# One total order of a sequence-mixing and dense kernel replaced by another

## The chip, the cores and the metric

The kernel runs on one core of one Trainium2 chip. The metric is the device time of one execution in microseconds, and of several runs the median. TensorE (PE in the profile, its weight loads PEld), VectorE (DVE), ScalarE (ACT), GpSimd (POOL) and SyncE (SP, which here only issues DMAs) each work through a list of instructions of their own; semaphores tie the lists together.

## The reference

One sequence of S = 2048 positions with D = 640 channels goes through a residual block with a long convolution, and then through a residual dense block with F = 1728 hidden columns. All inputs are bf16.

```python
def _A_ref(q, k, v, shift_k, ssm_k, ssm_D):       # q is layernorm(x)
    k_shift = sum of k moved down by t, times shift_k[:, 3 - t], t = 0..3
    kv = k_shift * v
    y = irfft(rfft(kv, 4096) * rfft(ssm_k, 4096))[:2048]    # along S, per channel
    y = y + kv * ssm_D
    return q * y

def _B_ref(x, w1, b1, w2):
    h = x @ w1 + b1
    return (h * tanh(softplus(h))) @ w2           # mish

x = A_q
h = x + _A_ref(_layernorm(x), A_k, A_v, A_shift_k, A_ssm_k, A_ssm_D)
h2 = h + _B_ref(_layernorm(h), B_w1, B_b1, B_w2)
return h2
```

## The kernel before

**How work is cut.** The code builds a list of 660 operations. Each has a name, the engines that may do it, the operations that it depends on and, if it writes PSUM, a buffer. A buffer is one of four banks of 128 x 1024 f32, and an operation that takes a bank must wait until the last reader of the bank's earlier contents is done. Nothing is planned at build time: the string `ORDER` at the top of the file holds every name once, in one total order. `s2kpe_84@3` means that the product s2kpe_84 writes bank 3; `y0:d` means that y0 is done by VectorE; a letter left out means the first engine that the operation allows. `_ordered` turns the string into the list that is emitted:

```python
for tok in ORDER:
    tok, _, slot = tok.partition("@")
    name, _, eng = tok.partition(":")
    o = by_name[name]
    o.eng = _LETTER[eng] if eng else o.engs[0]
    if o.psum is not None:
        o.psum.slot = int(slot)
```

Each engine gets its operations in this order and does them in this order; between engines only the semaphores count. So a place in the string decides three things: what stands ahead of an operation on its own engine, whose bank it waits for, and, for a DMA, what stands ahead of it on its queue.

**Head.** `d_dr`, `d_cst` and `d_sk` (L271, L269, L270) are three small loads that ACT issues: the filter's direct term, a table of constants, the shift filter. `warm` (L284) makes ACT load its activation table. `wm` (L292) is nine products on zeros on TensorE. `cfpe` (L304) spreads the shift filter over the partitions, a product that needs d_cst and d_sk; `coef` (L309) copies it and `wsh0` to `wsh3` (L317) make weights from it.

**Loads.** SP issues them (L325): `d_n` (five, the long filter ssm_k), `d_k`, `d_v`, `d_g` (eight pieces of a DFT table), `d_x` (four pieces of x), `d_t2m`, `d_a12`, `d_w10` to `d_w14` (rows of w1), and at L491 and below `d_w2a`, `d_w2b`, `d_w2c` (w2).

**The convolution** is a DFT made of products with small tables.
- The filter: `dadd` (L370, DVE or POOL) adds the direct term to sample 0, `k1pe` (L376) transposes one of five blocks, `k1ev` copies it out of PSUM.
- `s1kpe` (L396, L397), 5 x 4 of them, is the first DFT stage of the filter: 16 products of a weight tile of 64 columns each, half into partitions 0 to 63, half into 64 to 127. `s1kev` copies out. `s2kpe_f` and `s2kev_f` (L422) are the second stage, six frequencies a time, with weight tiles of 128 columns.
- The input: `ktpe` (L341), `ktev`, `ktsh` (L345) transpose k and move it; `kspe` (L357, L358) multiplies by the wsh and so shifts; `kv` (L362, DVE) multiplies by v. `s1vpe`, `s1vev`, then `s2v0pe`, `s2v1pe`, `s2v2pe` and their copies are the same two stages for kv.
- `sw` (L450) are ten DMAs from SBUF to SBUF that exchange the real and imaginary rows of the filter's spectrum; `pr` (L461, DVE) multiplies the two spectra.
- `i1pe` (L479) and `i1ev` are the first stage of the inverse. `i2a`, `i2b` (for token tiles 0 to 3, in two parts) and `i2pe` (L531) are the second, one for each of 16 tiles of 128 tokens.

All copies out of PSUM named `...ev` and `y` go through one helper, `ev`: L261 if ACT does them, L263 if DVE does.

**The first norm** of tile t is `ln1_t` (L510, L511, DVE: two partial statistics and their union), `ln1pt` (L515 to L517, POOL: add eps, power -1/2, product) and `lnxt` (L522 on ACT, or L524 on POOL).

**Between the two blocks**, for each tile t: `y` copies the convolution out of PSUM (128 x 640), `wb` (L538, DVE) multiplies by the normed x, `h` (L540) adds the residual, `bn` (L544, L545) takes the second norm's statistics, `pow` (L549, L550, POOL) its power, `hc` (L559, DVE) applies it. Then the tile is transposed: tiles 0 and 1 on TensorE (`trpe`, L569, and the copy `trev`), all others by a DMA transpose that SP issues (`tr`, L573). Seven buffers hold hc, so hc of tile t waits for the transpose of tile t - 7.

**The dense block** works in five units of 256, 256, 512, 512 and 512 tokens. `m1peu_f` (L598, and L605 for the last 64 columns of F) multiplies unit u by two 128-column chunks of w1; `hbu_f` (L620, ACT) is the mish on the way out of PSUM; `m2pet` (L663, and L671 for the last 64 rows of two tiles at a time) multiplies tile t by w2; `rest` (L688) adds the residual and `d_outt` (L692) stores. The last tile is done in two parts, m2pe15a and m2pe15b (L685 for the addition of its parts, of 384 and 256 columns). Unit u needs the transposes of all its tiles: unit 2 needs tr4 to tr7, unit 3 tr8 to tr11, unit 4 tr12 to tr15. `w2z` (L495, POOL) clears half of two rows of w2.

**DMAs of SP** go out in the order of the string, with eight semaphores in rotation: each waits for the landing of the one eight earlier.

The place of an operation in the whole string, seen on each engine, is what the change touches. On TensorE, 160 of 214 operations stand ahead of the first m1pe, and m1pe2_3 (the first product of unit 2, in both orders) has 180 ahead of it.

Of the kernel before, what the change touches and what calls it, by code (L numbers as in the profile page):

```python
# [30 lines left out]
ktpe0_3 ktpe0_2 s1kev1_2 ktpe2_0@3 ktpe2_3 ktpe2_2 d_v2 ktpe2_1 ktpe0_1 ktev2 ktpe1_0@1 ktev0:a ktpe1_1 ktpe1_3 ktpe1_2 s1kpe3_3@0 d_g5 ktev1 ktsh2
s1kpe4_0@3 s1kev3_3 s1kpe1_1@2 ktsh0 s1kev4_0:d d_v3 s1kpe4_2@1 wsh0 s1kev1_1 s1kpe3_0@0 s1kev4_2:d s1kpe2_3@3 s1kev3_0 d_g3 ktpe4_0@2 ktpe4_2 ktpe4_3
s1kev2_3 ktsh1 ktpe3_0@1 ktpe4_1 ktpe3_3 ktev4 ktpe3_1 ktpe3_2 s2kpe_6@0 s2kpe_12@3 ktev3 s2kev_6 kspe0_0@2 s2kev_12 s2kpe_18@0 kv0_0 ktsh3 kspe2_0@1
s2kev_18 ktsh4 s2kpe_42@3 kv2_0 kspe3_0@2 s2kev_42 s2kpe_96@0 kv3_0 s2kpe_24@1 s2kev_96 kspe4_0@3 s2kev_24 kspe1_0@2 kv4_0 s2kpe_108@0 kspe1_1@1 kv1_0
s2kev_108 s2kpe_72@3 kspe0_1@0 d_x1 s2kev_72 kv1_1 d_x0 s2kpe_66@2 s2kpe_102@3 s2kev_66 kv0_1 kspe4_1@1 s2kev_102 s2kpe_120@2 kv4_1 kspe3_1@0
s2kev_120 s2kpe_126@3 kv3_1 s2kpe_78@1 s2kev_126 s2kpe_0@2 s2kev_78 s2kpe_114@3 s2kev_0:d s2kpe_36@0 s2kev_114 s2kpe_54@1 s2kev_36:d s2kpe_84@2
s2kev_54 s2kpe_60@3 s2kev_84 ln1_0 kspe2_1@1 s2kev_60 s2kpe_48@0 kv2_1 ln1p0 s1vpe0_2@2 s2kev_48 s1vpe1_1@3 s1vev0_2:d s1vpe2_1@1 d_x2 s1vev1_1
s1vpe1_0@0 d_x3 s1vev2_1 s1vev1_0:d s1vpe4_3@2 s1vpe3_2@3 s1vev4_3 s1vpe0_0@1 s1vev3_2:d s1vpe2_2@0 s1vev0_0 s2kpe_90@2 s1vpe1_2@3 s1vev2_2 s2kev_90:d
s1vpe0_3@1 s1vev1_2 s1vpe1_3@0 s1vev0_3:d s1vpe0_1@2 s1vev1_3 s1vpe3_0@3 s1vev0_1:d s1vpe4_1@1 s1vev3_0 s2kpe_30@0 s1vev4_1:d s2v0pe_0@2 s2kev_30
s2v0pe_48@3 s2v0ev_0 ln1_1 sw1_0 s1vpe2_0@1 s2v0pe_64@0 sw1_1 s2v0ev_48 lnx0:p s1vev2_0:d s2v0pe_112@2 sw0_0 ln1p1 s2v0ev_64 sw4_0 s2v0pe_32@3  # L40
s2v0ev_112:d s2v0pe_80@1 sw3_1 s2v0ev_32 s1vpe3_1@0 lnx1:p sw0_1 ln1_2 s1vpe4_0@2 s2v0ev_80 sw3_0 s1vpe3_3@3 sw4_1 ln1_3 s1vev3_1 ln1p2 s1vpe2_3@1
sw2_0 s1vev4_0 s1vev3_3:d sw2_1 s1vpe4_2@0 lnx2:p s1vev4_2 s2v0pe_96@2 pr1_64 ln1p3 s2v0pe_16@3 s2v0ev_96 s2v2pe_32@0 s1vev2_3:d lnx3:p s2v0ev_16
s2v2pe_80@2 pr1_96 s2v2ev_32 s2v2pe_112@1 s2v2pe_64@3 s2v2ev_112 pr1_0 s2v2pe_48@0 s2v2ev_64 s2v2pe_0@1 pr0_96 s2v2ev_0 s2v2pe_16@3 pr1_32 s2v2ev_16
s2v1pe_96@1 pr0_64 s2v2ev_48 i1pe1_1@3 s2v2ev_80 s2v2pe_96@0 pr3_0 s2v1ev_96 i1pe1_2@2 pr3_32 i1ev1_1 s2v1pe_64@1 pr0_32 s2v2ev_96 s2v1pe_0@3 i1ev1_2
pr0_0 s2v1pe_32@0 s2v1ev_0 pr3_64 i1pe1_3@2 d_w14 s2v1ev_64 d_w10 i1pe0_2@3 pr3_96 d_w11 s2v1ev_32 d_w12 i1pe0_1@1 pr4_0 d_w13 i1ev1_3 d_t2m i1pe3_3@0
i1ev0_1 pr2_96 i1pe3_1@2 i1ev3_3 pr2_64 i1pe3_0@1 i1ev0_2 i1pe0_3@0 pr2_0 i1ev3_0 i1pe0_0@3 pr2_32 i1ev3_1 i1pe3_2@1 i1ev0_3 pr4_96 i1pe2_0@2 i1ev0_0
# [687 lines left out]
```

## Time and profile before

| | before |
|---|---|
| median of 3 runs | 225.16 us (225.13 to 225.98) |
| the profiled execution's span | 223.5 us |
| busy: PE / PEld | 214.0 us (96%) / 157.6 us (70%) |
| busy: DVE / ACT / POOL | 133.2 us (60%) / 133.0 us (59%) / 58.9 us (26%) |
| DMA moved | 30.98 MB, mean 139 GB/s |
| share of the chain that ended last | PE 70%, DVE 13%, DMA 9%, ACT 4% |

The busy time of an engine is the time in which it had an instruction at work. The chain that ended last follows from the last instruction back to whatever released each step. The shares are averages over very different stages: convolution first, dense block after about 99 us. So the views of a stage say more than this table.

### The profile page before, as it was taken

What the parts mean: (1) busy time and instruction counts of PE and PEld (TensorE: products, weight loads), DVE (VectorE), ACT (ScalarE), POOL (GpSimd) and SP (SyncE); (2) the same over time, 40 slices, a digit from 0 to 9 for tenths busy, and PEclk for the clock granted to TensorE, in tenths of its full rate; (3) what the DMA queues carried; (4) which work ended last, traced back from release to release, by engine and by line L of the source; (5) the groups of instructions that cost most, each with busy time, mean ns of one, the idle gap of its engine ahead of it and who ended that gap; (6) DMA issues with size and microseconds to landing.
All of it is one profiled execution on the core that took longest, in us unless ns stands there. A gap on an engine that the chain in (4) does not pass through costs nothing.

```text
span 223.5 us, 6119 instructions
## 1 busy us (share of the span) xinstructions
PE 214.0 (96%) x2645; PEld 157.6 (70%) x2650; DVE 133.2 (60%) x232; ACT 133.0 (59%) x182; POOL 58.9 (26%) x120
## 2 busy tenths in 40 slices
...
GB/s 181 390 413 409 412 374 121 143 239 93 375 415 69 258 331 290 124 0 62 1 0 62 84 123 91 118 0 0 3 0 59 59 3 0 0 56 6 76 54 49
DMA packets 19563, 30.98 MB, mean 139 GB/s; under 512 B 10704, under 2 KB 14928, under 8 KB 18768
## 3 DMA queue, kind: packets, MB, share of 16 engines
...
q8 instruction: 21, 0.34, 0.7%
q10 hardware_dynamic: 336, 0.12, 0.2%
...
q0 software_dynamic: 96, 0.00, 0.0%
...
## 4 chain that ended last, share of the span: by engine, by line
PE 70%; DVE 13%; DMA 9%; ACT 4%; issue 2%; SPq 1%; POOL 1%; DVEq 0%
PE ps L663 26%; PE ps L598 25%; DVE ks L461 6%; DMA ks<-in_B_w_dram 4%; DMA ks<-ks 3%; PE ps L396 3%; PE ps L422 3%; ACT uv L261 3%; DMA ks<-in_A_ssm_k_dram 3%; PE ps L341 2%; PE ps L376 2%; DVE ks L263 2%; PE ps L357 2%; DVE ra L362 1%; PE ps L397 1%
## 5 line engine op out<-in xcount | busy, mean ns | idle before, releaser
L620 ACT ACTIVATE ks<-ps,b1s 128x512 bf16<-128x512 f32 (+1 forms) x69 | 36.1, 610 | 42.8 <-PE ps L598 30.3
L663 PE MATMUL ps<-ks 128*128 128x320 bf16 (+2 forms) x420 | 58.4, 299 | 0.0
L598 PE MATMUL ps<-G 128*128 128x512 bf16 (+1 forms) x320 | 57.0, 336 | 0.3
L688 DVE TENSOR_TENSOR rb<-ps,rb 128x640 bf16<-128x640 f32 x15 | 11.7, 816 | 68.9 <-PE ps L671 66.5
L663 PEld LDWEIGHTS <-ks 128*128 128x128 bf16 x420 | 40.6, 98 | 17.2 <-issue 1.3
L598 PEld LDWEIGHTS <-G 128*128 128x128 bf16 x325 | 31.3, 98 | 24.4 <-issue 1.1
L261 ACT CAST uv<-ps 128x1024 bf16<-128x1024 f32 x49 | 45.2, 1197 | 0.0
L261 ACT CAST ks<-ps 128x960 bf16<-128x960 f32 (+3 forms) x49 | 39.8, 905 | 8.1 <-PE ps L397 5.0
L461 DVE TENSOR_TENSOR ks<-ks,uv 128x2048 bf16<-128x2048 bf16 x20 | 23.1, 1225 | 0.7 <-DMA ks<-ks 0.7
L422 PEld LDWEIGHTS <-G 128*128 128x128 bf16 x512 | 20.9, 96 | 3.1 <-issue 2.5
L479 PE MATMUL ps<-a_t,ks 128*128 128x128 bf16 x320 | 18.8, 219 | 0.4 <-DVE ks L461 0.3
L479 PEld LDWEIGHTS <-ks 128*128 128x128 bf16 x320 | 18.3, 113 | 0.7 <-DVE ks L461 0.6
L422 PE MATMUL ps<-uv,G 128*128 128x64 bf16 (+1 forms) x384 | 12.8, 186 | 1.8 <-ACT uv L261 1.8
L544 DVE BATCH_NORM_STATS2 st<-rb 128x6 f32<-128x320 bf16 x32 | 14.0, 478 | 0.1
L515 POOL TENSOR_SCALAR ve<-mv 128x1 f32<-128x1 f32 x16 | 4.7, 292 | 34.9 <-DVE mv L511 34.2
L510 DVE BATCH_NORM_STATS2 st<-rb 128x6 f32<-128x320 bf16 x32 | 13.7, 471 | 0.0
L263 DVE CAST uv<-ps 128x1024 bf16<-128x1024 f32 x11 | 12.9, 1204 | 0.1
L362 DVE TENSOR_TENSOR ra<-ps,rb 128x1024 bf16<-128x1024 f32 x10 | 11.9, 1222 | 0.7 <-PE ps L358 0.5
L524 POOL TENSOR_SCALAR ra<-rb,r,nmr 128x640 bf16<-128x640 bf16 x8 | 8.9, 1118 | 10.0 <-PE ps L397 9.3
L422 PE MATMUL ps<-ks,G 128*128 128x160 bf16 x128 | 11.2, 230 | 0.0
L396 PE MATMUL ps<-cst,ra 128*64 128x128 bf16 x160 | 10.6, 219 | 0.7 <-ACT uv L261 0.5
L263 DVE CAST ks<-ps 128x1024 bf16<-128x1024 f32 (+1 forms) x9 | 10.5, 1197 | 0.5 <-PE ps L422 0.3
...
## 6 DMA issues: line engine op xcount, KB each, us to landing
...
```

What stands on the lines that cost most here:

```text
L261: nc.scalar.copy(o, i)
L263: nc.vector.tensor_copy(o, i)
L362: nc.vector.tensor_tensor(kv_w[:, m, :, 8 * h:8 * h + 8, :], p_.f32().rearrange("p (l t d) -> p d t l", l=4, t=8), raw_v[:, 8 * h:8 * h + ...
L396: nc.tensor.matmul(ps[0:64, dgl, :], lhs, mc, start=True, stop=True)
L422: nc.tensor.matmul(p_.f32()[:, o:o + n], g_v[:, f, :], src[:, :, f, :], start=True, stop=True)
L461: nc.vector.tensor_tensor(o, o, v, ALU.mult)
L479: nc.tensor.matmul(pz[:, dgl, :], KS[:, k, b, :, l], a12[:, k, :], start=k == 0, stop=k == 1)
L510: nc.vector.bn_stats(st1[:, t, hh, :], xt(t)[:, hh * 320:(hh + 1) * 320])
L544: nc.vector.bn_stats(st2[:, t, hh, :], xt(t)[:, hh * 320:(hh + 1) * 320])
L598: nc.tensor.matmul(ph[:, o:o + w], w1[:, dc, fc * P:fc * P + P], lt[:, dc, 0:w], start=dc == 0, stop=dc == NDC - 1)
L620: nc.scalar.activation(hb[:, fc, 0:n], p_.f32()[:, i * 512:i * 512 + n], ACT.Mish, bias=b1s[:, fc:fc + 1], scale=1.0)
L663: nc.tensor.matmul(p_.f32()[:, o:o + n], lhs, w2[:, k, cols:cols + n], start=fc == 0, stop=single and fc == 13)
```

## The change

Only the string is exchanged. Both strings hold the same 660 names; every operation and its dependences stay. Of 660 operations 40 are done by another engine: 14 go from DVE to ACT, 19 from ACT to DVE, 3 from ACT to POOL (lnx4, lnx11, lnx12), 2 from DVE to POOL and 2 from POOL to DVE (four of the five dadd). 157 operations write another bank. Nearly every line of the string differs, so here are the stretches that matter below, each as the new string has it beside the old.

```diff
 ORDER = """
-d_dr wz idn d_n0 cz wm@0 small lane d_n1 d_cst d_sk d_n2 warm d_n3 d_n4 d_g0 dsel dcol dadd0 d_k2 k1pe0@1 d_k3 dadd1:p k1pe1@2 d_a12 k1ev0b d_k0 k1ev0
...
-s1kev1_3 kz b1pe@1 k1pe4@3 k1ev2 c_b1 cfpe@2 k1pe3@1 k1ev4:a coef d_v0 s1kpe2_0@0 k1ev3 wsh1 s1kpe2_1@2 s1kev2_0 s1kpe4_3@3 d_g7 s1kev2_1:d s1kpe3_1@1
...
-i1ev2_1 i1ev4_3:d i1pe4_2@0 i1ev4_0 lnx6:p i1pe4_1@2 ln1_4 i1ev4_2 ln1p11 i2a1@1 d_w2a i1ev4_1 ln1_14 i2a0@3 d_w2b ln1p4 d_w2c i2b1 ln1_10 i2a2@0 y1
-i2b0 i2pe4@2 y0 wb1 i2pe5@1 y4 h1 i2pe8@3 wb0 y5 h0 i2b2 i2a3@2 y8 bn1 i2pe15@1 y2 i2b3 i2pe12@3 bn0 y15 pow1 i2pe13@0 y3 i2pe11@1 pow0 y12 hc1 wb2
-trpe1@2 y11 i2pe7@3 hc0 y13 h2 trpe0@1 trev1:a wb3 i2pe6@0 bn2 trev0:a i2pe10@2 y7 m1pe0_3@1 h3 lnx11 pow2 bn3 m1pe0_2@3 y6 hc2 y10 pow3 ln1_7
-m1pe0_1@0 tr2 lnx8 ln1p10 hc3 hb0_3 m1pe0_5@2 wb8 tr3 hb0_2 h8 ln1p7 m1pe0_6@1 ln1_9 hb0_5 m1pe0_4@3 hb0_1 ln1p14 ln1_15 m1pe0_0@2 hb0_6 lnx4 wb6 w2z
-m1pe1_0@0 wb11 lnx10 wb4 lnx7:p hb0_4 m1pe1_4@1 ln1_5 ln1p15 hb1_0 m1pe1_5@3 wb7 hb0_0 h4 ln1p5 hb1_4 m1pe1_3@0 bn8 hb1_5 lnx5:p m1pe1_1@2 ln1_13
-hb1_3 pow8 m1pe1_2@1 wb5 hb1_1 h6 ln1p9 lnx15 m1pe1_6@3 bn6 hb1_2 h5 i2pe9@0 pow6 hb1_6 bn4 i2pe14@2 lnx9 ln1p13 m2pe0@1 hc6 ln1_12 y9 tr6 y14 lnx13:p
-bn5 lnx14 pow4 hc8 h11 pow5 tr8 m2pe1@3 wb14 h7 ln1p12 hc5 hc4 bn7 tr4 lnx12 wb10 pow7 tr5 bn11 m2pe2@0 h10 pow11 bn10 wb13 pow10 hc7 hc11 tr7 wb9
-wb15 m2pe3@2 res0 tr11 h9 hc10 d_out0 h14 tr10 h15 res2 bn9 d_out2 m1pe2_3@1 wb12 pow9 bn14 h12 pow14 m1pe2_6@0 hc9 hb2_3 bn15 tr9 hc14 h13 m1pe2_5@1
...
-m1pe4_1@3 hb4_0 m2pe9@2 hb4_1 m2pe11@0 m2pe8@1 res11 res9 d_out9 d_out11 m2pe10@3 m2pe15a@0 res10 res8 d_out8 m2pe12@2 res15a d_out15a d_out10
-m2pe14@3 m2pe13@1 res14 res12 d_out14 d_out12 m2pe15b@0 res13 d_out13 res15b d_out15b
+wz d_dr d_n0 idn wm@0 warm d_sk lane d_cst dsel cfpe@1 dcol cz dadd0:p coef d_n1 k1pe0@2 dadd1 k1pe1@3 wsh0 k1ev0 k1ev1 s1kpe0_1@0 d_n2 dadd2:p
...
+i1ev2_3 i1ev3_0:d i1pe2_1@0 ln1_2 i1pe4_2@1 i1ev4_2:d i1pe4_1@2 i1ev2_0 i1pe4_0@3 d_w11 i1ev2_1 ln1_1 i1pe4_3@0 ln1p2 ln1p1 i1ev4_1 i2a0@1 i2a1@2
+i1ev4_0 ln1_4 lnx1:p i1ev4_3 i2a3@3 i2b1 ln1_3 y1 ln1p3 i2b0 i2b3 y0:d i2pe8@0 i2a2@2 wb1 d_w2b d_w12 i2b2 wb0 d_w13 y3 h1 i2pe15@1 y8 i2pe13@3 h0 bn1
+i2pe5@0 d_w14 y2 lnx3:p bn0 lnx2:p pow1 y15 y5 wb3 pow0 hc1 i2pe10@2 i2pe4@1 y13 wb2 hc0 y4 i2pe6@0 i2pe11@3 ln1p4 i2pe12@1 y6 trpe1@0 y10 trpe0@2
+trev1:a h3 y12 trev0 h2 bn2 bn3 i2pe7@0 pow2 pow3 hc2 ln1_6 m1pe0_6@2 ln1p6 hc3 m1pe0_2@1 lnx6:p ln1_14 lnx4:p tr2 ln1_8 wb6 ln1_7 ln1_5 hb0_6 ln1_11
+wb4 tr3 y7 h4 ln1p8 hb0_2 m1pe0_5@2 m1pe0_4@0 m1pe0_1@1 hb0_5 h6 y11 ln1_12 w2z m1pe0_0@2 ln1p5 ln1p7 ln1_10 d_w2c m1pe0_3@3 hb0_4 hb0_1 lnx7:p hb0_0
+m1pe1_2@0 d_w2a ln1_15 ln1_13 ln1p11 m1pe1_5@1 m1pe1_3@2 lnx11:p lnx5:p bn4 wb7 ln1p15 wb5 ln1p14 h7 hb0_3 ln1p13 ln1p10 bn7 hb1_2 hb1_5 ln1_9 wb11
+lnx8 hb1_3 bn6 pow4 m1pe1_0@3 m1pe1_4@0 hb1_0 hb1_4 pow6 h5 m1pe1_1@1 hb1_1 m1pe1_6@2 i2pe9@3 pow7 ln1p12 hb1_6 i2pe14@0 lnx14 m2pe1@1 lnx15 bn5 wb8
+hc6 y14 wb15 pow5 hc4 lnx12:p lnx10 h8 wb10 h11 tr6 y9 hc5 m2pe0@2 lnx13:p ln1p9 h10 m2pe3@0 m2pe2@3 hc7 bn11 lnx9 bn10 tr4 bn8 pow11 res1 wb9 tr7 tr5
+d_out1 pow10 wb12 h9 res3 pow8 res2 hc11 tr11 wb13 m1pe2_3@1 hc10 m1pe2_2@0 bn9 hc8 pow9 m1pe2_5@3 wb14 h12 h13 hb2_3 res0 hb2_2 m1pe2_6@1 h15 tr8
...
+m2pe13@2 m2pe15b@1 d_out15a d_out10 d_out12 d_out9 res13 d_out11 res15b d_out13 d_out14 d_out15b
 """.split()
```

What stands ahead of the operations that the argument below comes back to, counted on each engine:

| | before | after |
|---|---|---|
| ACT: operations ahead of y1 | 86 | 83 |
| DVE: operations ahead of wb1, of them ln1 | 77, 10 | 76, 5 |
| TensorE: changes between weight tiles of 64 and 128 columns ahead of the dense block | 14 | 22 |
| POOL: from bn2 to the last statistics that unit 2 needs | 8 ln1p, 8 pow, 3 lnx, w2z | 10 ln1p, 6 pow, 5 lnx, w2z |
| SP: place of d_w2a | ahead of d_w2b | behind tr3 |

The places of the small loads: before, cst and the shift filter are issued ahead of the activation table load, and cfpe comes behind k1pe0, k1pe1, k1pe2 and k1pe4; after, they come behind `warm`, and cfpe ahead of all k1pe.

More of the change, by code (lines that the diff above doesn't have):

```diff
@@ L31 @@
[L31 to L46, printed above, removed]
@@ L55 @@
-wb15 m2pe3@2 res0 tr11 h9 hc10 d_out0 h14 tr10 h15 res2 bn9 d_out2 m1pe2_3@1 wb12 pow9 bn14 h12 pow14 m1pe2_6@0 hc9 hb2_3 bn15 tr9 hc14 h13 m1pe2_5@1
-tr14 hb2_6 bn12 res3 pow12 m1pe2_4@0 res1 d_out3 hb2_5 pow15 hc12 bn13 tr12 m1pe3_0@2 hc15 pow13 hb2_4 tr15 hc13 d_out1 tr13 m1pe2_0@3 hb3_0 m1pe3_2@1
-hb2_0 m1pe3_6@0 hb3_2 m1pe2_1@2 hb3_6 m1pe3_5@3 hb2_1 m1pe2_2@1 hb3_5 m1pe3_1@0 hb2_2 m1pe3_3@2 hb3_1 m1pe3_4@3 hb3_3 m2pe4@1 hb3_4 m2pe6@0 m2pe5@2
-res4 res6 d_out6 d_out4 m2pe7@3 m1pe4_2@1 res7 res5 d_out7 d_out5 m1pe4_5@0 m1pe4_6@3 hb4_5 hb4_2 m1pe4_4@2 hb4_6 m1pe4_3@0 hb4_4 m1pe4_0@1 hb4_3
@@ new lines @@
+d_k2 k1ev4:a k1pe3@2 k1ev3 s1kpe2_2@1 kz s1kpe0_0@0 s1kev2_2 d_k3 s1kpe2_3@3 wsh2 d_a12 wsh1 d_k0 s1kpe4_3@2 d_k1 d_g7 s1kpe4_1@1 s1kev0_0:d s1kev2_3
+s1kpe3_0@0 s1kev4_1 s1kev4_3:d s1kpe2_0@3 wsh3 s1kev3_0 s1kpe4_0@2 small s1kpe1_2@1 s1kev2_0:d ktpe2_0@0 ktpe0_0@3 d_g5 s1kev4_0 ktpe2_3 ktpe2_2
+ktpe2_1 d_v1 ktpe0_2 ktpe0_3 ktpe0_1 ktpe1_0@2 ktev2 ktpe1_2 ktpe1_1 s1kev1_2 ktpe1_3 ktpe4_0@1 ktev0:a d_g1 ktev1 s1kpe3_2@0 ktpe4_3 d_g6 ktpe4_2
+ktpe4_1 ktev4 s1kpe4_2@3 ktsh1 s1kev3_2 s1kev4_2 s1kpe0_2@2 s1kev0_2:d s1kpe0_3@0 s1kpe3_1@1 d_v0 s1kev0_3 s1kpe3_3@3 b1pe@2 s1kev3_1:d ktpe3_0@0
@@ new lines @@
+ktpe3_2 s1kev3_3 ktpe3_1 ktsh4 ktsh2 ktpe3_3 d_v2 c_b1 s2kpe_84@3 s2kpe_96@1 s2kev_84 ktev3 kspe4_0@2 ktsh0 s2kev_96 s2kpe_6@0 kspe2_0@3 kv4_0 kv2_0
+s2kev_6 s2kpe_102@1 d_v3 d_g2 s2kpe_24@2 kspe0_0@0 s2kev_102 s2kpe_18@3 s2kev_24 kspe0_1@1 kv0_0 s2kev_18 d_g4 d_g3 kv0_1 s2kpe_120@2 ktsh3 s2kpe_30@0
+s2kev_120 kspe3_1@3 s2kpe_78@1 kspe3_0@2 s2kev_30 s2kev_78 kv3_1 s2kpe_48@0 s2kpe_54@3 s2kev_48 kspe1_0@1 kv3_0 s2kev_54 s2kpe_12@2 kv1_0 d_x0
+kspe2_1@0 s2kpe_108@3 s2kpe_42@1 s2kev_12 s1vpe0_1@2 kv2_1 s2kev_108 s2kpe_72@0 kspe1_1@3 s1vev0_1:d s2kev_42 s2kpe_126@1 s2kev_72 s2kpe_0@2 kv1_1
```

18 lines of the change are left out of this document (15 added, 3 removed).

## The prediction

> **What bounds the kernel now.** I read the busy times by stage first, cut where the kind of work changes: loading and transposing (0 to 28 us), filter work and its copies out of PSUM (28 to 91.5), the step into the second layer norm (91.5 to 99.4), the dense layer as far as the first product of its third unit, m1pe2_3 (99.4 to 130.6), and the rest. The columns after the length are busy us and instructions of PE, PEld, DVE, ACT and POOL, then granted clock, DMA share and GB/s.
>
> ```profile
> 0.00:28.00 28.00, 25.96 (x459) 21.86 (x460) 17.80 (x26) 18.31 (x19) 14.04 (x28) 1.00 0.92 361
> 28.00:91.50 63.50, 59.81 (x1314) 56.33 (x1312) 61.43 (x75) 61.47 (x68) 16.34 (x30) 1.00 0.68 249
> 91.50:99.40 7.90, 7.32 (x59) 4.21 (x58) 6.77 (x19) 7.89 (x14) 2.33 (x6) 1.00 0.01 2
> 99.40:130.60 31.20, 31.20 (x263) 24.03 (x261) 28.06 (x77) 19.60 (x40) 21.84 (x47) 1.00 0.24 46
> 130.60:220.30 89.70, 89.44 (x558) 51.17 (x561) 18.74 (x38) 25.70 (x42) 4.31 (x10) 1.00 0.14 38
> ```
>
> From 28 to 91.5 us ACT and DVE are both busy 97% of the time: copying out of PSUM and the filter products set the pace there, and TensorE waits for a bank. From 99.4 us on TensorE has no gap (31.20 of 31.20, then 89.44 of 89.70). So three places decide: when the dense layer can start, whether its operands keep coming, and the tail. I then read the timeline at the seams. ACT's first copy y of the inverse transform stands at 91.51, the first product of the dense layer at 99.49, m1pe2_3 at 130.62.
>
> ```profile
> 91.51 1.29 ACT L261 CAST ks<-ps 128x640 bf16<-128x640 f32 x2 [0.36 <-DMA ks<-in_B_w_dram]
> 99.49 0.71 PE L598 MATMUL ps<-G 128*128 128x256 bf16 x5
> 126.20 0.80 DVE L559 TENSOR_SCALAR rw<-rb,mv,r 128x640 bf16<-128x640 bf16 x2
> 130.24 0.45 PE L671 MATMUL ps<-ks 64*128 64x320 bf16 x4
> 130.62 1.68 PE L598 MATMUL ps<-G 128*128 128x512 bf16 x6
> ```
>
> The 126.20 row is hc7 and hc11 on DVE: hc7 is the last normalisation that m1pe2_3 needs, and its DMA transpose lands just as TensorE gets there. That seam is tight already.
>
> **The change, part by part.** All operations stay, so no duration changes; only the order on each engine, the banks and 40 choices of engine do. I counted the operations ahead of the seams in both orders. Ahead of the dense layer's first product TensorE has 160 of its 214 operations either way, ahead of m1pe2_3 180 either way, of the same kinds. So TensorE's list behind each seam is equally long, and the end moves as m1pe2_3 moves, unless a new wait comes behind it.
>
> *The head.* cfpe (L304) goes ahead of the transposes of k1pe0, and ACT issues the loads that it needs behind the activation table load.
>
> ```profile
> 1.40 0.60 ACTq L269 DMA_DIRECT2D cst<-tab_cst  x1
> 2.03 0.45 ACTq L270 DMA_DIRECT2D sk_r<-in_A_shift_k_dram  x1
> 2.51 1.28 ACT L284 ACT_TABLE_LOAD   x1 [2.51 <-issue]
> 5.41 1.36 PE L376 MATMUL ps<-ident,ks 128*128 128x128 bf16 x16
> 7.20 1.20 PE L376 MATMUL ps<-ident,ks 128*128 128x128 bf16 x16 [0.42 <-DMA ks<-in_A_ssm_k_dram]
> cst<-tab_cst ACTq DMA_DIRECT2D x1, 104.0 KB, 4.3
> sk_r<-in_A_shift_k_dram ACTq DMA_DIRECT2D x1, 5.0 KB, 4.9
> ```
>
> The two loads are second and third on ACT's queue again, only exchanged, so the later is issued at about 2.0 and lands at 2.0 + 4.9 = 6.9. k1pe0 then starts at 6.9 instead of 5.41 and, at 1.1 each, k1pe1 ends at 9.1 instead of 8.4: 0.7 late. No row shows an ACT DMA behind a table load. From below 0.4 us (landing after 4.3, and the second transpose waits for its row until 7.20 anyway), from above 2.3 (both issues wait for 2.51 + 1.28 + 0.2 = 4.0, less the 1.4 at which the first could go, with the same landing times). I take 0.8, near the 4.9 row. In its own sentence: the Trainium skill, Trace Analysis, "Per-engine timelines", says that a compute instruction is pushed into a wait queue and leaves the sequencer free to go on; by that the issues are not held and the price is the lower one, and no row of this trace tests it, since here nothing is issued by ACT behind a compute instruction.
>
> *The copies.* What stands ahead of y1 on ACT shrinks from 86 operations to 83: three copies of 1024 columns fewer. By the 28 to 91.5 row one takes 61.47 / 68 = 0.90, so ACT has 2.7 us less. Ahead of wb1 DVE gives up five of its ten first-norm statistics ln1 and takes three copies and y0 instead.
>
> ```profile
> L461 DVE TENSOR_TENSOR ks<-ks,uv 128x2048 bf16<-128x2048 bf16 x20 | 23.1, 1225 | 0.7 <-DMA ks<-ks 0.7
> L263 DVE CAST uv<-ps 128x1024 bf16<-128x1024 f32 x11 | 12.9, 1204 | 0.1
> L510 DVE BATCH_NORM_STATS2 st<-rb 128x6 f32<-128x320 bf16 x20 | 8.5, 469 | 0.0
> L511 DVE BATCH_NORM_AGGREGATE mv<-st 128x2 f32<-128x12 f32 x9 | 1.9, 209 | 0.3
> ```
>
> One ln1 is 2 x 0.47 + 0.21 less overlaps, 1.05; a copy 1.17 busy; y0, which DVE does not do before, 0.7 by the final additions below: -5.2 + 3.5 + 0.7 = -1.0. The two hand bank and data to each other, so I take the mean, 1.85; the bounds are 1.0 (DVE alone) and 2.7 (ACT alone). Less the 0.8 of the head y1 comes 1.05 earlier, at 90.45.
>
> *The weight tile's shape.* The change names it, but ahead of the dense layer the passages between 64 columns (the stage-1 products, L396 and L397) and 128 grow from 14 to 22.
>
> ```profile
> 18.97 0.11 PEld L396 LDWEIGHTS <-ks 128*64 128x64 bf16 x1
> 19.00 0.11 PEld L397 LDWEIGHTS <-ks 128*64 128x64 bf16 x1
> 19.20 0.43 PEld L341 LDWEIGHTS ps<-ident,ra 128*128 128x128 f32 x3
> ```
>
> Loads follow each other at 0.03 here; across the change it is 0.20, so one costs 0.17 and eight more 1.4 us of TensorE. I price it at nothing, since from 28 to 91.5 TensorE waits for banks that ACT and DVE empty; if that cover is gone it costs up to 1.4. The Trainium skill, TensorEngine Tiling (Array Packing), "Key Properties", speaks against this change in the same way: a change of tiling mode, not of tile alone, drains the engine. The 0.17 agrees with that. By the rule without cover the time would be the last rival's.
>
> *The fetch of instructions.*
>
> ```profile
> q8 instruction: 21, 0.34, 0.7%
> L422 PEld LDWEIGHTS <-G 128*128 128x128 bf16 x512 | 20.9, 96 | 3.1 <-issue 2.5
> ```
>
> TensorE runs the same instructions, so as many are fetched. At most the 2.5 us of the costliest weight loads' idle time put down to nothing else could hide a fetch, and where I looked TensorE was waiting for a bank. I take no change, and bound it by 1 us either way.
>
> *From y1 to m1pe2_3.* Here the deferred work comes back. Between bn2 and the last statistics that m1pe2_3 needs, POOL now has, in this order, 10 triples ln1p (it was 8), 6 pairs pow, 5 lnx (it was 3; lnx4 and lnx11 leave ACT) and w2z, and pow5 stands last. Its rows between 98 and 126 us:
>
> ```profile
> L516 POOL TENSOR_TENSOR r<-ve,mhalf 128x1 f32<-128x1 f32 x8 | 4.9, 618 | 0.7
> L550 POOL TENSOR_TENSOR r<-ve,mhalf 128x1 f32<-128x1 f32 x8 | 4.8, 596 | 0.7
> L549 POOL TENSOR_SCALAR ve<-mv 128x1 f32<-128x1 f32 x8 | 2.8, 348 | 4.3 <-DVE mv L545 4.0
> L524 POOL TENSOR_SCALAR ra<-rb,r,nmr 128x640 bf16<-128x640 bf16 x3 | 2.6, 867 | 0.2
> L517 POOL TENSOR_SCALAR nmr<-mv,r 128x1 f32<-128x1 f32 x8 | 2.6, 320 | 0.8
> L515 POOL TENSOR_SCALAR ve<-mv 128x1 f32<-128x1 f32 x8 | 2.1, 258 | 0.3
> L495 POOL MEMSET ks<- 64x640 bf16 x2 | 1.2, 625 | 0.1
> 129.93 1.20 SPq L573 DMA_TRANSPOSE G<-rw  x1
> G<-rw SPq DMA_TRANSPOSE x14, 2.6
> ks<-in_B_w_dram SPq DMA_DIRECT2D x1, 2080.0 KB, 8.7
> ```
>
> Busy: 10 x (0.618 + 0.320 + 0.258) + 6 x (0.596 + 0.348) + 5 x 0.867 + 2 x 0.625 = 23.2. Between instructions, DVE's 4.0 left out, stand 3.1 us for 45 of them, 0.07 each; the new chain's 49 make 3.4: 26.6 in all. Counted from y1: ten y copies on ACT at 7.89 / 14 = 0.56 and a wait end at 6.2; trpe0, trev0 (now on DVE, 0.65), h2 and bn2 lead to pow2 at 8.9. 26.6 and 0.6 of waits for bn3 and ln1_6 give pow5 at 36.1; hc5, h10 and hc7 at 0.4 each and a start, 37.5; two transposes on SP, tr7 for 1.2 and then tr5 with 2.6 to its landing: **41.3**. On DVE three bn and res1, which frees m1pe2_3's bank, also end at 37.5 + 3 x 1.04 + 0.7 = 41.3. Before it is 130.62 - 91.51 = 39.1. TensorE would be there at 7.6 + 31.1 = 38.7 (its own list from the first dense product on), so it now waits 2.6. The wait has DVE and POOL in it, bounds: 38.7 (none) and 42.5 (the ln1p at their slowest, 1.7 each, in part).
>
> The big load d_w2a moves behind tr3 on SP: issued at 14 from y1, with 8.7 to land it is there before m2pe1 at 23.5, and a slip is swallowed by the wait. Of the four remaining w1 rows three now queue behind d_w2b, which waits for the last i1pe: landed about 6 from y1, needed at 7.6.
>
> *Behind m1pe2_3 and the tail.* tr8 to tr15 move with it; tr9, the latest, lands 52 from y1 and is needed at 56. The end is as before: m2pe13, m2pe15b, a small addition and d_out15b, with two more output issues ahead of it on SP, 0.35 each, which fit beside m2pe15b.
>
> ```profile
> 216.00 5.36 SPq L692 DMA_DIRECT2D out_dram<-rb  x4
> 219.05 0.82 DVE L688 TENSOR_TENSOR rb<-ps,rb 128x640 bf16<-128x640 f32 x1 [2.35 <-PE ps L663]
> 220.58 0.42 DVE L685 TENSOR_TENSOR rb<-ps,rb 128x256 bf16<-128x256 f32 x1 [0.70 <-PE ps L663]
> ```
>
> **Sum**: y1 -1.05, y1 to m1pe2_3 +2.2, rest 0: +1.15 on a span of 223.5. The median of the runs, 225.16, lies 1.6 above that span; I carry the difference over: 224.7 + 1.6 = **226.3**.
>
> **The rivals.** *POOL keeps up.* Under half of its busy time before is in quiet stretches, and if DVE leaves it alone its chain shrinks, TensorE finds every transpose landed and only the earlier y1 counts: 38.7 instead of 39.1 and -1.05 give -1.4, **223.7**; with the copies at their bound of 2.7 instead of 1.85, 222.9. For it: after 99.4 us TensorE has never waited. Against: the chain above has no idle time to give. It decides if pow5 ends under 33.5 from y1. *The loads behind the table load are held* until it is done: the head costs 2.3 instead of 0.8, **227.8**; it decides from cfpe later than 8 us. *The change doesn't do what it says*: the eight added changes of shape lie bare, in the stretches where ACT and DVE wait for a product, and take the gain ahead of y1: +1.4, **227.7**.
>
> **How the numbers follow.** My forecast 0.42, POOL keeps up 0.30, held loads 0.14, bare shape changes 0.14. A measurement of this kernel tells about 0.5% from no change, 1.13 us: up to 224.03 it is faster, from 226.29 slower. The forecast sits on that border: 0.21 of its chance counts as slower, 0.19 as the same, 0.02 as faster. POOL keeping up gives 0.18 faster and 0.12 the same; the other two together 0.21 slower and 0.07 the same. Faster 0.20, same 0.38, slower 0.42. The range reaches from the second case with the copies at their bound, 222.9, to just beyond the last two, 228.2.
>
> **What would show it.** y1 (the first ACT copy of 128x640) at 89.5 to 91.5 and cfpe at 6.5 to 7.2 confirm the first half; PE L598 with a wait of 1 to 3 us near 130 us, ended by a transpose or by L688, and POOL without a gap for some 27 us ahead of it, the second. No such wait makes the second case right; cfpe beyond 8 us the third. What would make all of it wrong is a wait behind m1pe2_3, which I have at none.

## The result, and the profile after

The new order takes 233.32 us (median of 4 runs, 232.26 to 236.13) where the old one takes 225.28 in the same set: the ratio is 1.034, 95% interval 1.031 to 1.037. One of the four, 236.13, counts as slow; the ratio rests on the other three, whose median is 232.92, and the runs below are compared with that. The forecast was 226.3 with a range up to 228.2. The profiled execution has a span of 231.1 us against 223.5.

First the new order by stage, cut at the same events as the table of before (first product of the second filter stage, y1, first dense product, m1pe2_3); the columns are those of the first table of the prediction. Behind it the same cut for the first two stages of the old order.

```profile
0.00:30.40 30.40, 26.67 (x451) 22.25 (x451) 19.17 (x27) 17.65 (x18) 14.57 (x29) 0.94 0.94 364
30.40:93.70 63.30, 60.02 (x1326) 56.79 (x1325) 59.16 (x61) 59.92 (x66) 5.01 (x12) 1.00 0.54 199
93.70:101.60 7.90, 7.01 (x56) 3.95 (x54) 6.75 (x19) 7.33 (x12) 7.06 (x13) 1.00 0.03 8
101.60:137.50 35.90, 31.64 (x263) 24.02 (x261) 31.09 (x86) 17.88 (x37) 29.07 (x60) 1.00 0.36 90
137.50:227.50 90.00, 89.54 (x554) 51.20 (x561) 22.33 (x48) 24.96 (x42) 4.17 (x10) 1.00 0.16 38
```

```profile
0.00:27.30 27.30, 25.26 (x450) 21.18 (x451) 17.10 (x26) 18.31 (x19) 14.04 (x28) 1.00 0.92 359
27.30:91.50 64.20, 60.51 (x1322) 57.01 (x1322) 62.13 (x75) 61.47 (x68) 16.34 (x30) 1.00 0.68 251
```

Read the lengths first. The head takes 30.4 us instead of 27.3; the convolution behind it 63.3 instead of 64.2; from y1 to the first dense product's first weight load 7.9 in both; from there to m1pe2_3 35.9 instead of 31.2, with TensorE busy for only 31.64 of it and POOL for 29.07, against 21.84 before. Behind m1pe2_3 nothing is lost: the last product starts 89.6 us later in both. So the 7.6 us of the span are 2.2 at y1 (93.73 against 91.51), 4.7 between y1 and m1pe2_3 (43.8 against 39.1) and 0.7 behind the last addition (below).

The second place is the one that the prediction named. These are rows of the new order's timeline, POOL and DVE ahead of m1pe2_3 and then TensorE:

```profile
130.61 0.57 POOL L550 TENSOR_TENSOR r<-ve,mhalf 128x1 f32<-128x1 f32 x1
131.18 2.12 POOL L524 TENSOR_SCALAR ra<-rb,r,nmr 128x640 bf16<-128x640 bf16 x2
131.22 1.02 DVE L559 TENSOR_SCALAR rw<-rb,mv,r 128x640 bf16<-128x640 bf16 x1 [1.12 <-POOL r L550]
132.55 0.92 DVE L559 TENSOR_SCALAR rw<-rb,mv,r 128x640 bf16<-128x640 bf16 x1
133.56 0.45 PE L671 MATMUL ps<-ks 64*128 64x320 bf16 x4
137.53 2.75 PE L598 MATMUL ps<-G 128*128 128x512 bf16 x11 [3.53 <-DMA G<-rw]
```

pow5 (the first row) ends the chain of POOL; DVE has waited 1.12 us for it; hc5 and hc7 follow, and TensorE stands still for 3.53 us until their transposes land. POOL has just gone on to lnx12 and lnx13, and beside these hc5 and hc7 take 1.02 and 0.92 us, twice the 0.45 of before.

The first place is the head. These are the longest rows of ACT's waits up to the first s2k product, of the old order (to 27.3 us) and then of the new (to 30.4): us in all, times, longest.

```profile
ACT ks L261 <- PE ps L397: 5.0, 1, 5.0
```

```profile
ACT ks L261 <- PE ps L397: 10.6, 4, 8.6
```

ACT has nothing to copy until 11.5 us instead of 9.0, and then three more gaps: the stage-1 products reach it late and singly. TensorE also runs at half clock for 3.4 us there; columns are length, busy, granted clock, DMA share, GB/s:

```profile
8.50:9.50 1.00, 1.00 (x18) 0.86 1.01 401
9.50:10.50 1.00, 1.00 (x12) 0.50 1.02 414
10.50:11.50 1.00, 1.00 (x17) 0.50 1.06 432
11.50:12.50 1.00, 1.00 (x11) 0.50 1.02 422
12.50:13.50 1.00, 1.00 (x26) 0.93 1.02 425
```

The rows behind it are those of ACT and of TensorE's first product with the new head:

```profile
1.40 1.28 ACT L284 ACT_TABLE_LOAD   x1 [1.40 <-PEq L718]
1.47 0.53 ACTq L270 DMA_DIRECT2D sk_r<-in_A_shift_k_dram  x1
2.03 0.45 ACTq L269 DMA_DIRECT2D cst<-tab_cst  x1
```

```profile
7.66 0.20 PE L304 MATMUL ps<-sk_r,cst 32*128 32x80 bf16 x1 [2.39 <-DMA cst<-tab_cst]
```

The end: from the last addition to the end of the span are 3.2 us, before 2.5. Output issues of the last 8 us, new order: eight, with a median of 4.0 us to landing for the six whole tiles, where the old order's last ones take 1.8.

```profile
out_dram<-rb SPq DMA_DIRECT2D x6, 160.0 KB, 4.0
out_dram<-rb SPq DMA_DIRECT2D x1, 96.0 KB, 1.6
out_dram<-rb SPq DMA_DIRECT2D x1, 64.0 KB, 1.9
```

### The profile page after: what moved, and what is told of

Its sections match the earlier page's. It is cut to its first block, busy times and chain, and to the rows that moved or that the text cites. A ratio compares the mean times of both kernels' runs of the same rounds, so it can differ in the third digit from the quotient of the medians.

```text
span 231.1 us, 6122 instructions
## 1 busy us (share of the span) xinstructions
PE 214.9 (93%) x2643; PEld 158.2 (68%) x2650; DVE 138.9 (60%) x237; ACT 127.7 (55%) x174; POOL 59.9 (26%) x123
## 4 chain that ended last, share of the span: by engine, by line
PE 59%; DVE 14%; POOL 13%; DMA 7%; issue 4%; SPq 1%; ACT 1%; ACTq 0%; POOLq 0%; DVEq 0%
PE ps L663 19%; PE ps L598 18%; PE ps L422 6%; DVE ks L461 5%; DMA ks<-ks 3%; POOL ra L524 3%; POOL r L516 3%; PE ps L396 3%; PE ps L376 3%; DVE uv L263 3%; DMA cst<-tab_cst 2%; PE ps L341 2%; DVE ks L263 2%; POOL nmr L517 2%; PE ps L357 2%
## 5 line engine op out<-in xcount | busy, mean ns | idle before, releaser
L598 PE MATMUL ps<-G 128*128 128x512 bf16 (+1 forms) x318 | 57.6, 336 | 4.7 <-DMA G<-rw 4.2
L663 PE MATMUL ps<-ks 128*128 128x320 bf16 (+2 forms) x420 | 58.5, 299 | 0.0
L663 PEld LDWEIGHTS <-ks 128*128 128x128 bf16 x420 | 40.8, 98 | 17.3 <-issue 0.8
L261 ACT CAST uv<-ps 128x1024 bf16<-128x1024 f32 x46 | 42.7, 1058 | 1.8 <-PE ps L422 1.3
L263 DVE CAST uv<-ps 128x1024 bf16<-128x1024 f32 x14 | 16.6, 1216 | 0.3 <-ACT ks L261 0.2
L524 POOL TENSOR_SCALAR ra<-rb,r,nmr 128x640 bf16<-128x640 bf16 x11 | 10.6, 965 | 18.5 <-issue 17.9
L422 PE MATMUL ps<-uv,G 128*128 128x64 bf16 (+1 forms) x384 | 12.6, 187 | 1.9 <-issue 1.2
L396 PE MATMUL ps<-cst,ra 128*64 128x128 bf16 x160 | 11.0, 219 | 1.3 <-ACT uv L261 0.7
L263 DVE CAST ks<-ps 128x1024 bf16<-128x1024 f32 (+2 forms) x10 | 11.4, 1162 | 0.2
L397 PE MATMUL ps<-cst,ra 128*64 128x128 bf16 x160 | 11.3, 221 | 0.0
```

What stands on the lines that cost most here:

```text
L261: nc.scalar.copy(o, i)
L263: nc.vector.tensor_copy(o, i)
L396: nc.tensor.matmul(ps[0:64, dgl, :], lhs, mc, start=True, stop=True)
L422: nc.tensor.matmul(p_.f32()[:, o:o + n], g_v[:, f, :], src[:, :, f, :], start=True, stop=True)
L524: nc.gpsimd.tensor_scalar(lnx_s[t % 9], xt(t), r1[:, t:t + 1], nmr1[:, t:t + 1], ALU.mult, ALU.add)
L598: nc.tensor.matmul(ph[:, o:o + w], w1[:, dc, fc * P:fc * P + P], lt[:, dc, 0:w], start=dc == 0, stop=dc == NDC - 1)
```

## The experiments

Theories to be told apart: **the chain of POOL** sets m1pe2_3, against DVE's list or the freeing of the bank; **the head** carries through to y1, against copies out of PSUM that swallow it; and within the head, cfpe alone, POOL's queue, or the order of the stage-1 products. Edits are to the string, one name to a line. Where the total is disturbed by the granted clock (it falls in some executions, see below), the seams in the trace decide.

**The three row passes back on ACT**

```diff
-lnx4:p
+lnx4
-lnx11:p
+lnx11
-lnx12:p
+lnx12
```

> The new order with lnx4, lnx11 and lnx12 back on ACT, nothing else. Theory (POOL's chain sets m1pe2_3, and POOL's row work beside hc5 and hc7 makes these twice as long): pow5 loses two lnx of 0.94 ahead of it, hc5 and hc7 lose some 0.5 each, m1pe2_3 comes 2.5 to 3 us earlier, 233.3 becomes about 230.5. Rival (DVE's list or the freeing of the bank sets it): 0 to 1 us earlier, 232.3 or more.

Measured: 237.0 us, ratio 1.052 (1.047 to 1.056). Slower by 4.1 than the new order, so the edit that shortens POOL's chain misses. pow5 does start 3.0 us earlier (127.3). But ACT works in order, and lnx11 waits there for its statistics from POOL. ACT, from the timeline of this kernel, and then TensorE:

```profile
116.45 0.92 ACT L522 ACTIVATE ra<-rb,nmr,r 128x640 bf16<-128x640 bf16 x1 [7.86 <-POOL nmr L517]
```

```profile
118.15 6.16 PE L598 MATMUL ps<-G 128*128 128x256 bf16 x35 [5.15 <-ACT ks L620]
```

The mish passes behind lnx11 wait 7.86 us with it, their banks stay full, and TensorE stops for 5.15 us. Around this stop the granted clock falls as well:

```profile
115.00:120.00 5.00, 1.85 (x9) 0.58 0.27 91
120.00:125.00 5.00, 5.00 (x39) 0.74 0.00 0
```

m1pe2_3 comes 47.7 us behind y1 instead of 43.8; the half clock, which lasts to 122.65 in this profile, makes some 2.2 us of it (an estimate: half of the 4.5 us from the end of the stop on). So lnx11 on POOL was no loss by itself: with POOL's order as it is, ACT does it only at the price of the mish behind it. This run doesn't tell the theories apart.

**Two statistics moved behind pow5 on POOL**

```diff
-ln1p13
...
-ln1p12
 pow5
+ln1p12
+ln1p13
```

> The new order with ln1p13 and ln1p12, which unit 2 doesn't need, moved on POOL to behind pow5; no engine changes. Theory (POOL's chain): pow5 comes 2 x 1.7 = 3.4 us earlier, and m1pe2_3 as much: about 229.9. Rival (DVE's list sets it): under 1 us.

Measured: 229.91 us, ratio 1.020 (1.017 to 1.024), 3.0 less than the new order. y1 to m1pe2_3 is 40.3 us instead of 43.8, 3.5 less, with nothing changed in the order of DVE, ACT, SP or TensorE: pow5 ends 34.5 us behind y1 instead of 37.45, and hc5 and hc7 are back at 0.43, since lnx12 and lnx13 now come after them. The chain of POOL stands; DVE's list as the cause falls.

**The head's two releases**

```diff
+d_cst
+d_sk
 warm
...
-cfpe@1
...
 k1pe1@3
+cfpe@1
...
 k1ev1
+coef
+wsh0
```

> The new order with the head put back: the loads of the table of constants and of the shift filter ahead of the activation table load, in the old order, and cfpe behind k1pe1. Theory (the head costs what k1pe0 comes late, and it carries through to y1): k1pe0 at 5.4 instead of 7.8, no stretch at half clock, y1 2 us or more earlier, about 231. Rival (the stage behind is bound by the copies out of PSUM and swallows the head): y1 within 0.5 us of 93.7, time about 233.

Measured: 236.91 us, ratio 1.052 (1.044 to 1.059). k1pe0 starts at 5.18 and there is no half clock in the head, as expected, and yet y1 comes at 94.16, 0.4 later. TensorE's rows for k1pe2 show what took over, and POOL's row says why:

```profile
10.39 1.09 PE L376 MATMUL ps<-ident,ks 128*128 128x128 bf16 x15 [1.52 <-DVE coef L309]
12.81 0.27 PE L376 MATMUL ps<-ident,ks 128*128 128x128 bf16 x1 [1.33 <-POOL ks L370]
```

```profile
10.42 2.06 POOL L317 TENSOR_TENSOR rw<-cst,coef 128x1120 bf16<-128x1120 bf16 x1 [4.80 <-DVE coef L309]
```

k1pe2 first waits for bank 1, which cfpe filled and coef empties, and its last transpose for dadd2, which the new order gives to POOL behind wsh0 (2.06). In the new order both covers lie behind the late cfpe and aren't seen. The rest of the total is the clock: behind the wait at m1pe2_3 it fell in this execution, and the row of the stretch reads

```profile
135.00:140.00 5.00, 2.06 (x5) 0.65 0.42 98
140.00:145.00 5.00, 5.00 (x17) 0.67 0.39 67
```

m1pe3_2 then stands 17.3 us behind m1pe2_3 instead of 14.6.

**The output issues**

```diff
 res9
+d_out10
+d_out9
+d_out11
...
 res14
+d_out12
+d_out15a
+d_out14
...
-d_out15a
-d_out10
-d_out12
-d_out9
 res13
+d_out13
-d_out11
 res15b
-d_out13
-d_out14
 d_out15b
```

> The new order with the output issues of tiles 9, 10, 11, 12 and 14 pulled ahead, so that behind the last product only those of 13 and 15b are left. Theory (the burst of eight issues at the end delays the last): from the end of the last addition to the end of the span 2.5 us instead of 3.2, time 0.7 us less, 232.6. Rival: no change.

Measured: 235.68 us, ratio 1.046 (1.043 to 1.048), with the clock down behind m1pe2_3 in the same way (2.8 us by the distance to m1pe3_2). The step itself is as expected: 2.5 us from the last addition to the end, where the new order has 3.2, and the outputs land after a median of 1.8 again. That the burst alone costs this isn't shown, though: e8_warm15 and e10_head_only, below, keep it and have 2.5 us too, their six whole tiles landing after a median of 2.6 and 1.9, and e15_fit_tr3, without it, has 4.2 in its profile.

**Both covers of the head, on top of the relief of POOL.** e2_pow5 with the edit of e3_head, and

```diff
-dadd2:p
+dadd2
-dadd3:p
+dadd3
```

> e2_pow5 (229.9) with the head of e3_head and besides dadd2 and dadd3 back on DVE, so that neither stands behind wsh0 (2.05 us) on POOL. Theory (two covers lie on the head: cfpe ahead of k1pe0, and dadd2 behind wsh0 ahead of the last transposes of k1pe2; e3_head took away only the first): k1pe2 done at about 10 instead of 12.9, the first s2k product 2 to 2.5 us earlier than the 29.85 of e2_pow5, y1 as much, time about 227.5. Rival (the head is swallowed by the copies whatever releases it): first s2k product within 0.7 us, time about 229.5.

Measured: 229.68 us, ratio 1.018 (1.016 to 1.021). The first s2k product comes 0.3 us earlier (29.56) and y1 0.5 (92.48). The rival has it right, but not by its reason: k1pe2 still waits 1.52 us for the bank that coef empties, and there is only one stage-1 product ahead of it to copy meanwhile, where the old order has five.

**The waits behind the seam.** e2_pow5 with the output issues of e4_tail, and

```diff
 pow5
+ln1p9
...
+tr5
 tr7
-tr5
```

> e2_pow5 (229.9) with three waits behind the seam taken away: ln1p9 directly behind pow5 on POOL (wb9 waits for it on DVE, and res3, which frees the bank of m1pe2_2, stands behind wb9), tr5 ahead of tr7 on SP, and the output issues of e4_tail. Theory: m1pe2_3 0.4 us earlier, m1pe2_2 1.0 us, the tail 0.6 us, in all 2 us: 227.9. Rival (the wait at m1pe2_2 is for something else): 0.6 to 1 us, about 229.

Measured: 228.62 us, ratio 1.013 (1.010 to 1.016), 1.3 less than e2_pow5. By the trace: y1 to m1pe2_3 40.1 (0.2 less), m1pe2_3 to m1pe3_2 14.6 instead of 15.6 (the wait at m1pe2_2 is gone), last addition to end 2.5 instead of 3.2. Together 1.9, as expected; y1 itself was later in this execution (94.39), with the half clock in its head and once more from 62.9 to 66.3 us.

**All of these together**

> e5_head2 and e6_seam_tail together. If both theories hold and their gains add: 229.9 less 2.5 less 2 gives 225.4, what the kernel before takes, with y1 near 90.5, a us earlier than before. Rival (the head's gain is used up ahead of y1): 227.5 or more.

Measured: 227.4 us, ratio 1.009 (1.007 to 1.011); y1 at 92.78. The gains behind y1 add; the one ahead of it isn't there, as e5_head2 had shown.

**TensorE kept busy at the start**

```diff
-WARM = 9
+WARM = 15
```

> e2_pow5 with 15 products on zeros at the start instead of 9, which keep TensorE busy until k1pe0 starts; nothing else. Theory (the idle stretch of 2.5 to 3 us ahead of k1pe0 is what halves the granted clock between 9.4 and 12.6 us in some runs, and this costs what the profile of the new order shows against that of e2_pow5, 0.7 us at y1): granted clock 1.00 from 0 to 20 us in every run, and the median 0 to 0.7 us less than 229.9. Rival (the clock falls for another reason): the dip stays.

Measured: 228.78 us, ratio 1.014 (1.011 to 1.017), 1.1 less than e2_pow5. The mean granted clock of its four executions is 1.000, 1.000, 1.000 and 0.998; of e2_pow5 1.000, 0.991, 0.990 and 0.993. So the clock stays up where the idle stretch ahead of cfpe (2.4 us in the new order's profile, 1.6 in that of e2_pow5) is filled. That the 1.1 us come from it isn't shown: the profiled spans are equal (227.9), y1 comes later than in e2_pow5 (93.64 against 92.97), the tail is shorter (2.5 against 3.2), and executions of one kernel lie about 2 us apart here.

**The old head, three times.** The first 127 operations (all ahead of the first s2k product) in the old order with its banks and engines, then the new order: on e7_all, and on the new order itself; and the other way round, the new head ahead of the old order.

> e7_all (227.4) with everything up to the first s2k product in the order, the banks and the engines of before (127 operations), then the new order for the rest, with the mends of e7_all. Theory (the head loses its 2.3 us not at cfpe but by its order of stage-1 products: four that could run beside the wait for the third filter block stand behind k1pe2, and the copies on ACT start late): first s2k product at 27.4 instead of 29.6, y1 at 90.5, m1pe2_3 at 130.5, time 225.2, as before. Rival (the rest can't use an earlier start, since the loads and exchanges set it): y1 within 0.7 us of 92.8, time about 227.

> The new order with the old head alone (the same splice, none of the other mends). Theory: first s2k product at 27.4, y1 at 90.5, but y1 to m1pe2_3 stays at 43.8, m1pe2_3 at 134.3 and the time 230, or 3 us more where the granted clock falls in the wait at m1pe2_3. Rival: y1 within 0.7 us of 93.7, time 233.

> The kernel before with the new head alone: the first 123 operations in the new order, then the old order. Theory: first s2k product at 29.9 to 30.4, y1 2.5 to 3 us later than 91.5, m1pe2_3 39.1 behind it, time 228. Rival (the head is swallowed by the copies): time 225.5 to 226.

Measured: 233.96 (1.037, 1.034 to 1.041), 239.11 (1.061, 1.056 to 1.066) and 230.08 us (1.020, 1.015 to 1.025). In the third y1 comes at 96.91, 5.4 later than in the old order; it is taken again below with other loads. The first two were spoilt by what the splice did to SP: the new rest begins its second stage with frequency 84, the old head loads that piece of the table late. TensorE's wait in e9_head_before, us in all, times, longest:

```profile
PE ps L422 <- DMA G<-tab_g: 5.4, 1, 5.4
```

One thing in e10_head_only is clean: with y1 at 97.26, m1pe2_3 comes 43.8 us behind it, as in the new order. What happens behind y1 doesn't depend on the head.

**The heads exchanged, with the loads in the sequence that the rest wants**

> e9_head_before with one thing more: the table and v loads go out on SP in the new order's sequence (7, 5, v1, 1, 6, v0, v2, v3, 2, 4, 3), since the new s2k order begins with frequency 84. Theory (the head's 2.3 us lie in its order of stage-1 products, and e9 lost time only by the table piece that came late): first s2k product at 27.4 to 27.7, no wait for the table above 1 us, y1 at 90.5 to 91, m1pe2_3 at 130.5 to 131, time 225.2 to 225.7. Rival (the loads, not the products, pace the new order ahead of 36 us, so an early start only waits): y1 at 92 or more, time 226.7 or more.

> e11_before_newhead with the table and v loads in the old sequence, which the old s2k order wants. Theory: first s2k product at 29.9 to 30.4 and y1 2.5 to 3 us behind the 91.51 of before, at 94.0 to 94.5, time 228: the new head alone costs what it is late. Rival: the later start is made up where the engines wait for loads, y1 at 92 to 92.5, time 226 to 226.5.

Measured: 227.82 us (1.011, 1.008 to 1.014) and 229.66 us (1.019, 1.015 to 1.022). In the second, in front of the old order, the new head brings the first s2k product of that order (s2kpe_6) at 31.37 instead of 27.34, y1 at 95.45 instead of 91.51, m1pe2_3 still 39.1 behind it. What the head is late goes through to the end. Of these 3.9 us, 1.5 are the joint (TensorE waits there for a bank that DVE's copies of k empty), so the head itself makes some 2.5. In the first the old head is ready at 27.32, but the joint wastes it: s2kpe_96 waits for the bank that ktpe3 fills last in the old head, and y1 comes at 92.27.

```profile
29.39 0.58 PE L422 MATMUL ps<-ks,G 128*128 128x160 bf16 x6 [1.38 <-DVE uv L263]
```

**The joint fitted**

```diff
-s2kpe_96@1
+s2kpe_96@0
...
-kspe4_0@2
+kspe0_0@2
...
-kv4_0
+kv0_0
...
-kspe0_0@0
+kspe4_0@1
...
-kv0_0
+kv4_0
```

(and banks 0 and 1 exchanged in all that follows)

> e12_head_loads (227.8) with the joint of the two orders fitted: banks 0 and 1 exchanged in the rest (there s2kpe_96 waited 1.4 us for the bank of ktpe3, which the old head empties last) and kspe4_0 and kv4_0 exchanged with kspe0_0 and kv0_0 (the old head has the shifted copy of block 0 ready first). Theory (the old head is worth 2.3 us, and the joint of e12 took most of it): the first kspe at 28.3 instead of 29.7, y1 at 90.9, time 226.4. Rival (what is left is the new rest's own pace): y1 within 0.4 us of 92.3, time 227.5 or more.

Measured: 226.08 us over 12 runs, ratio 1.003 (1.000 to 1.005). y1 at 91.28, 0.2 earlier than in the old order and 1.5 earlier than in e7_all; m1pe2_3 at 131.33, and TensorE no longer waits for a transpose in front of it. With the old head, POOL relieved and the tail mended, the new order takes the time of the old within 0.5%. It doesn't beat it.

The seams of the profiled executions side by side, in us:

| | first s2k product | y1 | m1pe2_3 | y1 to m1pe2_3 | span |
|---|---|---|---|---|---|
| before | 27.34 | 91.51 | 130.62 | 39.1 | 223.5 |
| after | 30.44 | 93.73 | 137.50 | 43.8 | 231.1 |
| e2_pow5 | 29.85 | 92.97 | 133.24 | 40.3 | 227.9 |
| e5_head2 | 29.56 | 92.48 | 133.06 | 40.6 | 227.5 |
| e7_all | 29.57 | 92.78 | 132.77 | 40.0 | 225.7 |
| e14_head_fit | 27.61 | 91.28 | 131.33 | 40.1 | 224.3 |

**Tile 3's transpose earlier.** e14_head_fit with

```diff
-trev0
+trev0:a
...
+hc3
 ln1_6
-hc3
```

> e14_head_fit with trev0 back on ACT and hc3 ahead of ln1_6 on DVE, so that the transpose of tile 3 goes out earlier (m1pe1_2 waits about 0.9 us for it in the new order). Theory: 0.4 to 0.8 us less than e14_head_fit, where m1pe2_3 then waits for TensorE's own list and not for its transposes: about 225.8. Rival (m1pe2_3 waits for POOL's chain all the same): the same time as e14_head_fit.

Measured: 226.73 us over 12 runs, ratio 1.005 (1.002 to 1.008). No gain; m1pe2_3 comes 40.3 us behind y1, in e14_head_fit 40.05. The theory fails; what is left between y1 and m1pe2_3 isn't that transpose. Executions of both kernels lie 3 us apart, so less than half a us stays open.

## Why the prediction was wrong, point by point

It had the mechanism of the largest loss, and missed the sign and size of what stands ahead of y1. Its sum was y1 -1.05 (head +0.8, copies -1.85), y1 to m1pe2_3 +2.2, rest 0. Measured: y1 +2.2 (head +3.1, copies -0.9), +4.7, +0.7. The head and the chain of POOL were each taken more than 2 us too small, the copies 1 us too large, and the tail at nothing.

- **The head, forecast 0.8 late, measured 3.1 at the first s2k product: the step that failed.** It priced the head by when k1pe0 and k1pe1 end, through cfpe and its loads. That was near: the two loads go out at 1.47 and 2.03, beside the table load (1.40 to 2.68), so they aren't held. The rule of the Trainium skill cited there (Perfetto Trace Analysis, "Per-engine timelines": a compute instruction leaves the sequencer free) agrees with these rows. But the second load takes 5.6 us to land, not 4.9, and k1pe0 starts at 7.8, not 6.9. What it didn't count is what is copied next. Five stage-1 products stand ahead of k1pe2 in the old order, one in the new, and ACT idles 5.6 us more (1.1 of it only because its table load is done that much sooner). At y1 the head is worth 2.45: 0.8 from the new order's profile to that of e2_pow5, in which the half clock is missing and the table of constants lands 0.8 sooner, 0.5 for the two releases (e5_head2), and the remaining 1.2 up to e14_head_fit, which sets the old head whole, its order of the stage-1 products with it. No run took that order alone. In front of the old order the new head costs 3.9 with the joint, some 2.5 without (e13_newhead_loads).
- **The copies, forecast 1.85 earlier.** Up to y1 ACT's busy time did fall by 2.2 us and DVE's by 0.9, near the 2.7 and 1.0 that were counted; between the first s2k product and y1 it fell by 1.5 and 3.0. But only 0.9 of it became time, just under the lower bound of 1.0; measured from the same head (e14_head_fit, 63.7 us against 64.2) it is 0.5. A busy share of 97% was read as a rate at which less work is less time; it isn't, once the order makes one engine wait for the other, and TensorE's own idle time in this stretch, all that faster copies could win, was only 3.7 us before and is 3.3 after. What fills the gap isn't settled. The eight added changes of shape, priced at nothing, are a candidate, and no run took them alone; but only four of them lie in this stretch, 0.7 us at the prediction's 0.17 each. The trace shows a second one. These are rows of TensorE's waits in this stretch, of the old order and then of the new:

```profile
PE ps L422 <- ACT uv L261: 1.8, 7, 0.3
PE ps L531 <- ACT uv L261: 0.8, 1, 0.8
```

```profile
PE ps L422 <- issue: 1.2, 2, 0.7
PE ps L422 <- ACT uv L261: 0.6, 3, 0.2
PE ps L396 <- issue: 0.3, 1, 0.3
```

The waits for banks shrink, and 1.5 us appear for which the profile names no cause ("issue"); the old order has none of these. Each of these three waits ends 1.3 to 1.5 us behind the landing of a block of instructions (the blocks land at 55.15, 60.97 and 67.82 us by the trace's DMA records), and from wait to wait TensorE's records count exactly 256 instructions. e7_all and e14_head_fit have the same three waits with the same count. That points to late instructions, a term that the prediction took at nothing and bounded by 1 us; no run tested it.
- **y1 to m1pe2_3, forecast +2.2, measured +4.7.** Place, engines and releaser are as forecast: POOL without a gap, pow5 last, then hc5, hc7 and the transposes. pow5 came 37.45 behind y1 instead of 36.1: pow2 0.9 later than reckoned, since lnx3 and lnx2 stand ahead of pow1 on POOL, and the chain 27.6 instead of 27.2. hc5 and hc7 took 1.02 and 0.92 instead of 0.45 beside POOL's row passes, and the rest is 0.2 in the landing. e2_pow5 showed the chain by taking 3.5 off it.
- **The tail, forecast 0.** "Fit beside m2pe15b" was wrong: with eight outputs in a burst d_out15b is issued 0.3 us behind the last addition, before at its end, and lands 1.9 later instead of 1.5. Without the burst the 0.7 is gone (e4_tail, e6_seam_tail), but so it is in two profiles that keep the burst (e8_warm15, e10_head_only); why it costs something in one execution and not in another stays open.
- **Right**: the list behind m1pe2_3 is as long as before (89.6 us to the last product); d_w2a's move costs nothing (no product of L663 waits); as many instructions are fetched (21 packets).
- **Not thought of**: that the granted clock falls where TensorE has waited. It added 2.7 and 2.8 us in the profiles of e3_head and e4_tail. The runs of the new order spread over 4 us; the slowest has the lowest mean clock (0.985), but the clock doesn't order the other three (0.993, 0.993 and 1.000 from the fastest up).
- **The rivals.** *Loads held* named the head, at 227.8, but by a hold that isn't there; *POOL keeps up* fell; *bare shape changes* stays untested. The range failed because it let one term at a time go wrong, and all four did, the same way.
